# Decode attention: the first weight load is one of 16 rows on partitions 0 to 15

## The chip, the cores and the metric

The kernel runs on one core of one Trainium2 chip. The metric is the time of one execution in microseconds of device time. The median of three runs before the change was 1265.98 us (1265.68 to 1267.26).

## The reference

One token is decoded. Its row x of 448 numbers is used in two branches, which a gate mixes. Branch a is attention with a long cache: 16 query heads of 256 over 8 key/value heads with 65536 positions each. Branch b is a small MLP over a layer-normed x. All tensors are bf16.

```
g = sigmoid(sum(x * gate_w))
q = x @ wq                                  # 448 -> 16 heads of 256
p = softmax(q . k / 16)                     # two query heads share one key head, 65536 positions
a = (p @ v) @ wo                            # 4096 -> 448
u = gelu(layernorm(x)^T * w1 + b1)          # 448 x 1792
b = u @ w2 + b2
out = g * a + (1 - g) * b
```

The two caches are 268 MB each; everything else is under 8 MB. So nearly all traffic is keys and values, each of which is read once.

## The kernel before, in words

The work goes in 32 passes (`NP`), four for each key/value head. A pass covers 16384 positions: 8 MB of keys and 8 MB of values, laid out as 128 partitions of 64 KB. Keys go into `kring`, values into `vbuf`.

SyncE (`block.sync`) issues all large loads in one hand-written order, with waits on semaphores that say when a buffer is free. The DMA engines take its queue, q1, in that order. TensorE turns the keys of a pass around in 128x128 blocks (line 349, into the PSUM tile `kst`), ScalarE (line 797) and VectorE (line 657) copy the result to `ktT`, and TensorE multiplies it by the current query `qcur` (line 370). After the maxima and the exponentials, the values are summed up with the weights `pT` (line 401).

Ahead of the passes there is a short prologue. SyncE's first issues, in this order, are:

- line 256 (`load_wo(0)`): the output weights of the first key/value head, 128 rows of 3.5 KB, into `wo_sb`;
- line 259: `wq_a`, the first 384 rows of the query weights. Partition p gets rows 3p to 3p+2, one run of 24 KB;
- line 261: `wq_b`, the remaining 64 rows, as 128 runs of 4 KB;
- line 264, twice: the second and then the first half of the first keys, 128 runs of 32 KB each.

ScalarE issues six small loads on its own queue, q10: x, the gate weights, three parameter vectors of the MLP, and one bias. TensorE waits for both loads of query weights (`sem_wq`, line 490) and computes all queries (lines 497 and 499). `wq_a` and `wq_b` lie in the space of `vbuf`, so SyncE holds the first values back (lines 272 and 273) until the query projection and the broadcast of the layer-normed row are through. The output weights are first read after the fourth pass (line 462).

Of the kernel before, what the change touches and what calls it, by code (L numbers as in the profile page):

```python
# [12 lines left out]
def bass_gated_mix__gqa_block_cached__mixer_token_mlp__decode_kernel(  # L13
# [25 lines left out]
    P = 128  # L39
# [17 lines left out]
    WF = 3  # L57
# [38 lines left out]
    with ctx:  # L96
# [6 lines left out]
        def new_sem(name):  # L103
            return ctx.enter_context(nc.semaphore(name))
# [22 lines left out]
        wq_a = early[:, 0:WF * NQ].rearrange("p (j n) -> p j n", j=WF)  # L127
# [75 lines left out]
        sem_wq = new_sem("sem_wq")  # L203
# [43 lines left out]
        def src(cache, j, n0=0, n1=NV):  # L247
            g, m = divmod(j, PPH)
            s = cache[0, g, m * BODY * CH:(m + 1) * BODY * CH, :].rearrange("(p n) d -> p n d", p=P)
            return s[:, n0:n1, :].rearrange("p n d -> p (n d)")  # L250

        @block.sync
        def _(eng):
            def load_wo(g):
                w = A_wo[g * REP * DH:(g + 1) * REP * DH, :]
                eng.dma_start(wo_rows, w.rearrange("(p i) n -> p (i n)", i=2 * REP)).then_inc(sem_wo, 16)

            load_wo(0)
            eng.dma_start(wq_a.rearrange("p j n -> p (j n)"),
                          A_wq[0:WF * P, :].rearrange("(p j) n -> p (j n)", p=P)).then_inc(sem_wq, 16)  # L260
            eng.dma_start(wq_b, A_wq[WF * P:DM, :].rearrange("r (a n) -> (r a) n", a=2)
                          ).then_inc(sem_wq, 16)
            def load(dst, cache, j, n0, n1, at, sem):
                eng.dma_start(dst[:, at + n0:at + n1, :].rearrange("p n d -> p (n d)"), src(cache, j, n0, n1)  # L264
                              ).then_inc(sem, 16)

            load(kring, A_k_cache, 0, HV, NV, 0, sem_k)
            load(kring, A_k_cache, 0, 0, HV, 0, sem_kb)

            def load_v(j):  # L270
                if j == 0:
                    eng.wait_ge(s_q, 1)
                    eng.wait_ge(s_hb, 1)
                else:
                    eng.wait_ge(sem_pv, j)
                load(vbuf, A_v_cache, j, 0, NV, 0, sem_v)
                g, m = divmod(j, PPH)
                if m == 0 and 1 <= g < H - 1:
                    eng.wait_ge(s_proj, g)
                    load_wo(g)  # L280

            for j in range(NP):
                if j == LEAD + 1:
                    eng.wait_ge(sem_tr[NB - 1], BODY * LEAD)
                    load(kring, A_k_cache, j, HV, NV, HV, sem_kc[1])
                if j >= 1:
                    eng.wait_ge(sem_tr[NB - 1], BODY * (j - 1) + DC)
                if j == LEAD:
                    load(kring, A_k_cache, j, HV, NV, 0, sem_k)
                    load(kring, A_k_cache, j, 0, HV, 0, sem_kc[0])  # L290
                elif j == LEAD + 1:
                    load(kring, A_k_cache, j, 0, HV, HV, sem_k)
                elif j == NP - 1:
                    load(kring, A_k_cache, j, 0, HV, HV, sem_k)
                    load(kring, A_k_cache, j, HV, NV, HV, sem_kc[2])
                elif j >= 1:
                    load(kring, A_k_cache, j, 0, NV, HV * (j % 2), sem_k)
                if j < LEAD:
                    load_v(j)
                elif j > LEAD:  # L300
                    load_v(j - 1)


            for (n0, n1), sem in zip(pieces, sem_vp):
                if n0 == 0:
                    eng.wait_ge(sem_tr[NB - 1], BODY * (NP - 1))
                elif n0 == NRING:
                    eng.wait_ge(sem_pv, NP - 1)
                load(kring if n1 <= NRING else vbuf, A_v_cache, NP - 1, n0, n1, 0, sem)
            eng.wait_ge(s_proj, H - 1)  # L310
            for h in range(REP):
                w = A_wo[(HQ - REP + h) * DH:(HQ - REP + h + 1) * DH, :]
                eng.dma_start(wo_sb[:, h, :], w.rearrange("(p j) n -> p (j n)", j=2)).then_inc(sem_wl[h], 16)
            eng.wait_ge(s_fin, NCG)
            eng.dma_start(out_ap, out_row[:, :]).then_inc(sem_out, 16)
            eng.wait_ge(sem_out, 16)
# [13 lines left out]
        def _(pe):  # L330
# [95 lines left out]
            def piece_wait(n):  # L426
                for (n0, _), sem in zip(pieces, sem_vp):
                    if n == n0:
                        pe.wait_ge(sem, 16)
# [57 lines left out]
            pe.matmul(acc[:, WF + 2:WF + 2 + 3 * FT], wrows_b, identb, start=True, stop=True).then_inc(s_col, 1)  # L487

            pe.wait_ge(s_xcol, 1)
            pe.wait_ge(sem_wq, 32)  # L490
            for dj in range(2):
                for h in range(HQ):
                    j = dj * HQ + h
# [28 lines left out]
            with nc.Fori(0, NP + 1, 1, engines=on, head_slot={pe.engine: 0}) as jj:  # L522
                j = pe.snap(jj, min_val=0, max_val=NP)
# [312 lines left out]
```

## Time and profile before

| | |
|---|---|
| median of 3 runs | 1265.98 us |
| profiled execution: time / span | 1266.13 us / 1264.3 us |
| moved by DMA | 544.39 MB, mean 431 GB/s over the span |
| TensorE busy | 956.9 us (76%), mean granted clock 0.856 |
| ScalarE / VectorE busy | 544.5 us (43%) / 497.4 us (39%) |
| first query projection matmul | 12.97 us |
| first transposes of keys (line 349) | 24.04 us |
| first values issued by SyncE | 17.9 us |
| first output projection (line 462) | 202 us |

The time of an execution includes what lies outside of the span of instructions (1.8 us here). "Issue to landing" of a load runs from the moment that SyncE issues it to the moment that its semaphore is complete, so it includes the time that it stands behind earlier loads.

### The profile page before, as it was taken

The page shows a single profiled execution, that of the slowest core. Times are in us where ns is not written, and L with a number is a line of the kernel's source. Part 1 is how long each engine was busy: PE and PEld are TensorE (multiplying, and loading weights), DVE is VectorE, ACT ScalarE, POOL GpSimd, SP SyncE. Part 2 cuts the span into 40 slices and gives each one's busy share as a digit, 9 for nine tenths or more (in the row PEclk, how much of TensorE's full clock was granted, in tenths as well). Part 3 has the DMA queues.
Part 4 walks back from the last instruction along what each step waited for, and adds up shares of the span by engine and source line. Part 5 has one row for each costly group of instructions (what it writes and reads, how often), then busy time and mean ns, then how long its engine had stood idle before and what let it go on. Part 6 is the DMA issues. An engine that isn't in the chain of part 4 may idle for free.

```text
span 1264.3 us, 39978 instructions
## 1 busy us (share of the span) xinstructions
PE 956.9 (76%) x17201; PEld 881.7 (70%) x17201; DVE 497.4 (39%) x1125; ACT 544.5 (43%) x692; POOL 0.9 (0%) x7
## 2 busy tenths in 40 slices
PE   4778887678776787767877768886769867697786
PEld 3677876668766687666877667775668756687674
DVE  3333434444544444444344423342333423344342
ACT  2444543345533455334554334443344533345451
POOL 0000000000000000000000000000000000000000
PEclk9878887898888897788988889887888878898898
DMA  9999999999999999999999999999999999999998
GB/s 421 427 421 422 438 435 433 438 431 431 431 433 440 433 433 431 431 440 431 433 433 424 438 440 433 431 427 433 433 435 440 423 435 431 435 433 435 427 446 353
DMA packets 12055, 544.39 MB, mean 431 GB/s; under 512 B 1417, under 2 KB 1676, under 8 KB 2956
## 3 DMA queue, kind: packets, MB, share of 16 engines
q1 hardware_dynamic: 11954, 544.22, 99.7%
q8 instruction: 8, 0.13, 0.0%
q10 hardware_dynamic: 90, 0.01, 0.0%
q14 instruction: 3, 0.02, 0.0%
HBM read 544.22 MB, written 0.00 MB: 430 GB/s over the span
## 4 chain that ended last, share of the span: by engine, by line
DMA 63%; PE 34%; issue 1%; DVE 1%; DVEq 0%; SPq 0%; ACT 0%
DMA kring<-in_A_k_cache_dram 59%; PE kst L349 25%; PE sps L370 6%; DMA vbuf<-in_A_v_cache_dram 2%; PE acc L401 2%; DMA wo_sb<-in_A_wo_dram 1%; PE acc L451 0%; PE sps L389 0%; SPq L264 0%; PE acc L394 0%; DVE ktT L657 0%; PE sps L387 0%; ACT z_b L802 0%; DVE mrow L668 0%; DVE accs L691 0%
## 5 line engine op out<-in xcount | busy, mean ns | idle before, releaser
L349 PE MATMUL kst<-ident,kring 128*128 128x128 f32 x4096 | 557.2, 297 | 196.9 <-DMA kring<-in_A_k_cache_dram 173.1
L349 PEld LDWEIGHTS kst<-ident,kring 128*128 128x128 f32 x4096 | 505.5, 154 | 205.4 <-issue 199.9
L797 ACT ACTIVATE ktT<-kst 128x1024 bf16<-128x1024 bf16 x512 | 499.0, 1021 | 345.2 <-PE kst L349 344.5
L657 DVE COPY ktT<-kst 128x1024 bf16<-128x1024 bf16 x512 | 353.8, 692 | 440.3 <-PE kst L349 414.4
L370 PEld LDWEIGHTS sps<-qcur,ktT 128*128 128x128 bf16 x8192 | 237.8, 96 | 2.6
L370 PE MATMUL sps<-qcur,ktT 128*128 128x2 bf16 x8192 | 236.6, 163 | 0.0
L401 PE MATMUL acc<-vbuf,pT 128*2 128x256 bf16 x4024 | 158.3, 332 | 6.1 <-DMA vbuf<-in_A_v_cache_dram 3.4
L401 PEld LDWEIGHTS acc<-vbuf,pT 128*2 128x2 bf16 x4024 | 110.7, 101 | 45.8 <-issue 5.7
L780 ACT ACTIVATE fade<-mdif 128x2 f32<-128x2 f32 x32 | 6.5, 204 | 301.1 <-DVE mdif L674 301.1
L668 DVE TENSOR_REDUCE mrow<-sps 2x1 f32<-2x128 f32 x32 | 8.9, 279 | 158.9 <-PE sps L387 158.9
L387 PE MATMUL sps<-ident,mcol 128*2 128x128 f32 x32 | 8.9, 279 | 29.9 <-issue 23.4
L389 PEld LDWEIGHTS sps<-mdiag,mones 2*128 2x128 f32 x64 | 11.4, 221 | 27.9 <-DVE mdiag L670 27.9
L784 ACT ACTIVATE pT<-sps,mneg 128x64 f32 x128 | 30.4, 335 | 0.0
L389 PE MATMUL sps<-mdiag,mones 2*128 2x2 f32 x64 | 14.1, 288 | 21.3 <-DVE mdiag L670 21.3
L394 PE MATMUL acc<-pT,ones_sq 128*128 128x32 bf16 x256 | 11.9, 182 | 22.8 <-issue 19.3
L387 PEld LDWEIGHTS sps<-ident,mcol 128*2 128x2 f32 x32 | 2.6, 80 | 37.8 <-issue 28.1
L802 ACT ACTIVATE z_b<-z_b 128x448 bf16<-128x448 bf16 x14 | 8.1, 578 | 48.1 <-DVE z_b L644 48.1
L691 DVE COPY accs<-acc 128x288 f32<-128x288 f32 x8 | 3.7, 458 | 62.3 <-PE acc L401 62.3
L663 DVE TENSOR_REDUCE mcol<-sps 128x2 f32<-128x256 f32 x32 | 13.5, 423 | 35.4 <-PE sps L370 35.4
L394 PEld LDWEIGHTS acc<-pT,ones_sq 128*128 128x128 bf16 x256 | 8.8, 99 | 26.1 <-issue 22.5
L686 DVE TENSOR_SCALAR acc<-acc,fader 128x256 f32<-128x256 f32 x32 | 15.8, 493 | 2.5
L673 DVE TENSOR_SCALAR mneg<-sps 128x2 f32<-128x2 f32 x32 | 5.1, 160 | 17.1 <-PE sps L389 17.1
(108 smaller groups left out, 171.1 us busy)
## 6 DMA issues: line engine op xcount, KB each, us to landing
kring<-in_A_k_cache_dram SPq DMA_DIRECT2D x8, 4096.0 KB, 23.7
kring<-in_A_v_cache_dram SPq DMA_DIRECT2D x1, 3584.0 KB, 35.9
wo_sb<-in_A_wo_dram SPq DMA_DIRECT2D x7, 448.0 KB, 25.7
vbuf<-in_A_wq_dram SPq DMA_DIRECT2D x1, 3072.0 KB, 10.3
vbuf<-in_A_v_cache_dram SPq DMA_DIRECT2D x1, 2560.0 KB, 9.2
vbuf<-in_A_v_cache_dram SPq DMA_DIRECT2D x1, 1024.0 KB, 11.3
vbuf<-in_A_v_cache_dram SPq DMA_DIRECT2D x1, 768.0 KB, 12.8
vbuf<-in_A_wq_dram SPq DMA_DIRECT2D x1, 512.0 KB, 11.1
```

The lines of the kernel that those rows point to most:

```text
L349: ins = pe.transpose(kst[:, b, i * P:(i + 1) * P], kring_f[:, at + NT * (k % DC) + 4 * b + i, :], ident[:, :])
L370: ins = pe.matmul(sps[:, 0, 2 * (NT * k + nt):2 * (NT * k + nt) + 2], ktT[:, par, b, ntl * DH + dj:(ntl + 1) * DH:2], qcur[:, dj, :], star ...
L387: pe.transpose(mxT, mcol[:, :], ident[:, :]).then_inc(s_mT, 1)
L389: pe.matmul(mxB, mones[:, :], mdiag[:, :], start=True, stop=True).then_inc(s_mB, 1)
L394: pe.matmul(acc[:, DENC:SELC], ones_sq[:, :], pT[:, r, :], start=False, stop=(r == BODY - 1), skip_group_check=True)
L401: ins = pe.matmul(acc[o:o + REP, 0:DH], pT[:, r, 2 * nt:2 * nt + 2], buf[:, n, :], start=False, stop=False, skip_group_check=True)
L657: vec.tensor_copy(ktT[:, k % KTB, b, :], kst_b[:, b, :]).then_inc(sem_ev[b], 1)
L663: vec.tensor_reduce(out=mcol[:, :], in_=scores_all.rearrange("p (n hh) -> p hh n", hh=REP), axis=AX.X, op=ALU.max)
L668: vec.tensor_reduce(out=mrow[:, :], in_=mxT, axis=AX.X, op=ALU.max)
L686: vec.tensor_scalar(acc[:, 0:DENC], acc[:, 0:DENC], fader[:, :], None, op0=ALU.mult).then_inc(s_acc, 1)
L784: ins = act.activation(pT[:, bass.ds(p0, DC), hh:2 * NT:REP], scores_all.rearrange("p (a r n hh) -> p a hh r n", a=2, r=DC, hh=REP)[:, hal ...
L797: act.activation(ktT[:, k % KTB, b, :], kst_b[:, b, :], AF.Copy).then_inc(sem_ev[b], 1)
```

## The change

The load of `wq_a` is divided by partitions. The rows of partitions 0 to 15 (16 runs of 24 KB) are issued first of all. Then come the output weights, unchanged, and then the rows of partitions 16 to 127 (112 runs of 24 KB). All that follows keeps its order. `sem_wq` counts one load more, so TensorE waits for 48 instead of 32. Bytes, destinations and all other engines' programs stay as they are.

```
-            load_wo(0)
-            eng.dma_start(wq_a.rearrange("p j n -> p (j n)"),
-                          A_wq[0:WF * P, :].rearrange("(p j) n -> p (j n)", p=P)).then_inc(sem_wq, 16)
+            for p0, p1 in ((0, 16), (16, P)):
+                eng.dma_start(wq_a[p0:p1].rearrange("p j n -> p (j n)"),
+                              A_wq[WF * p0:WF * p1, :].rearrange("(p j) n -> p (j n)", j=WF)).then_inc(sem_wq, 16)
+                if p0 == 0:
+                    load_wo(0)
             eng.dma_start(wq_b, A_wq[WF * P:DM, :].rearrange("r (a n) -> (r a) n", a=2)
                           ).then_inc(sem_wq, 16)
...
-            pe.wait_ge(sem_wq, 32)
+            pe.wait_ge(sem_wq, 48)
```

## Prediction, made before the changed kernel had run

> **What bounds the kernel now.** I read the page's slices and DMA queues first, to see which resource is never idle. The columns of a queue line are packets, MB, and share of 16 engines.
>
> ```profile
> DMA  9999999999999999999999999999999999999998
> GB/s 421 427 421 422 438 435 433 438 431 431 431 433 440 433 433 431 431 440 431 433 433 424 438 440 433 431 427 433 433 435 440 423 435 431 435 433 435 427 446 353
> ...
> q1 hardware_dynamic: 11954, 544.22, 99.7%
> ```
>
> The 16 DMA engines are busy in every slice, and nearly all that they move is SP's queue, q1. Then I read stretches of the span (length, busy time and instructions of each engine, granted clock, DMA share, GB/s).
>
> ```profile
> 24.00:118.00 94.00, 72.02 (x1206) 65.44 (x1206) 32.43 (x62) 41.08 (x50) 0.00 (x0) 0.84 1.01 433
> 118.00:121.00 3.00, 2.64 (x49) 2.63 (x49) 1.38 (x2) 1.61 (x3) 0.00 (x0) 1.00 0.87 328
> 121.00:1240.00 1119.00, 863.40 (x15507) 800.22 (x15503) 452.03 (x1008) 497.27 (x630) 0.00 (x0) 0.86 1.00 433
> ```
>
> From 121 to 1240 us the share is 1.00 at 433 GB/s: 27.06 GB/s for each engine. TensorE is busy for 863.4 of those 1119 us, so it is not the bound. Only at 118 to 121 us do the queues run short (0.87, or 0.13 x 3 = 0.4 us of stream). The waits between 30 and 1260 us say the same from the other side: TensorE waits for keys, 28 times.
>
> ```profile
> ...
> PE kst L349 <- DMA kring<-in_A_k_cache_dram: 167.3, 28, 9.7
> ...
> ```
>
> So the end is: when the stream starts, plus bytes over 433 GB/s, plus a tail of 2.5 us (the chain of waits has the last landing at 1261.8 us, the span ends at 1264.3). The tail is not touched, nor is a byte added. What the change can do is shift the stream as a whole, and the place to read is its first few microseconds. Here are SP's issues, then the DMA of the first 4 us in slices of 0.1 us.
>
> ```profile
> 0.74 0.41 SPq L256 DMA_DIRECT2D wo_sb<-in_A_wo_dram  x1
> 1.20 0.41 SPq L259 DMA_DIRECT2D vbuf<-in_A_wq_dram  x1
> 1.67 0.42 SPq L261 DMA_DIRECT2D vbuf<-in_A_wq_dram  x1
> 2.13 0.97 SPq L264 DMA_DIRECT2D kring<-in_A_k_cache_dram  x2
> ```
>
> ```profile
> DMA  0000000000000000097924598899889999950000
> GB/s 0 0 0 0 0 0 0 0 0 0 0 0 0 0 0 0 9 179 143 251 72 143 215 358 323 287 394 394 287 358 430 466 1162 1837 983 246 0 0 0 0
> ```
>
> The first packets move in slice 17 (1.7 us), 1.0 us after the issue. Slices 17 to 30 are the output weights (128 rows of 3.5 KB, 459 KB): their figures add up to 3834, times 0.1 us is 383 KB in 1.4 us, where 433 GB/s would have moved 606 KB. This stuttering start costs 223 KB / 433 GB/s = 0.5 us. (A packet's bytes are counted where it starts, hence the peaks behind it.)
>
> **The change part by part.** *One more issue on SP.* An issue takes 0.41 us and the next follows 0.46 us later, so the remaining query weights, the remainder load and both key loads are issued 0.46 us later than now. Cover: key bytes cannot move before some 4.1 MB ahead of them (9.5 us at 433 GB/s) have gone, and they are issued at 2.13 us. Cost 0; without that cover, 0.46 us. The 16 rows go where the output weights stood at 0.74 us, so the stream's first packet stays at about 1.7 us.
>
> *Output weights moved behind the 16 rows.* Their first reader is the projection at 202 us. Cost 0.
>
> *What the stuttering start gives back.* Sixteen rows of 24 KB give each engine one packet of 24,576 B / 27.06 GB/s = 0.91 us, under which the small rows can be prepared. The gain lies between 0 (any first packet is as slow) and 0.5 us (all of it). I take half: -0.25 us.
>
> *The 16 rows as a load on partitions 0 to 15.* All loads of q1 in the trace write 128 partitions, so they can't say whose limit 27.06 GB/s is: the engine's, or that of the eighth of a 128-row load (8 partitions) that each engine fills. If it is the engine's, the 16 rows take 0.91 us and cost nothing. If it is the destination's, what counts is how many such groups of eight the partitions 0 to 15 reach: 16 groups if neighbours are spread as widely as possible (0.91 us, +0), 2 if neighbours lie together (8 rows in turn, 7.3 us, +6.4). Dealt evenly, which I assume, each engine has one of these rows first in its queue, so all 16 are held up, and what stands behind them waits. Neighbouring partitions are nearer to the dense end than to the spread one: I take 4 groups, 4 rows in turn, 3.64 us, +2.73 us.
>
> [...]
>
> *The other 112 rows.* [...] With the destination as the limit, two engines that meet in a group take 1.82 us for a row each instead of 0.91. Ends: they never meet (+0), or each of the seven rows meets another (+6.4 us). Four groups have lost 4 of their 8 rows to the first load, so the other twelve still hold 8 where the even share is 7: one row, 0.91 us, is lost at the least. [...] I take three meetings for the later engines, since a load lands with its slowest engine: +2.73 us.
>
> [...]
>
> *Who waits for this.* The semaphore threshold of 48 is the same wait for one load more. TensorE starts the query projection at 12.97 us; 5 us later it would end at 21.6 instead of 16.6, and SP would issue the first values at about 23 instead of 17.9 us. The keys ahead of them keep the engines busy until about 11 + 19.4 = 30.4 us (8.39 MB at 433 GB/s), later still when shifted. Cover 12 us; if it were gone, each us late would cost one. ScalarE's small loads take turns with these packets and may land some us later than 11.4; their chain ends in the same projection. TensorE's first transposes, at 24.04 us, wait for the first half of the keys and move with the stream.
>
> *Sum.* -0.25 + 2.73 + 2.73 = +5.2 us. The stream is full from there to the end, so nothing gives it back, except up to the 0.4 us of 118 to 121 us, which itself hangs on transposes that start with a key landing and so moves too. The profiled execution took 1266.13 us (span 1264.3), which becomes 1271.3; it lies 0.15 us above the median of 1265.98, so I forecast 1271.2 us. A measurement of this kernel can tell about 0.2%, 2.5 us, from no change.
>
> **Rivals.**
>
> *The limit is the engine's own (chance 0.19).* Then both loads go at 433 GB/s wherever they land, and what is left is the start: 0 to -0.5 us, 1265.7 us, not slower. For it: the rate is the same for every load in the trace. Against it: nothing in this trace, since no large load there writes fewer than 128 partitions. It decides if the 16 rows are through by about 2.9 us.
>
> *Only the 16 rows suffer (0.16).* If the 112 rows are dealt so that engines hardly meet, -0.25 + 2.73 = +2.5 us, 1268.5 us, right at the 0.2%; half of this I count as slower. It includes the case that the loads are not dealt one row and seven rows to an engine: 16 rows on four engines, four each, would also hold those four up by 2.73 us.
>
> *Dense groups (0.06).* Two groups instead of four: +6.4 for the first load and 2 to 4 for the second, 1274 to 1276 us.
>
> *The change hides anyway.* A delay of the first loads would vanish if TensorE were the bound later. Its idle time before the transposes (167.3 us, ended by the keys) speaks against it: the only slack is 0.4 us. It is inside the first rival's range.
>
> *Faster by over 0.2% (0.03).* All that there is to gain is 0.5 us of the start and 0.4 us at 118 us, together 0.07%; only something that the trace doesn't show would give more.
>
> **How the numbers follow.** The forecast's own case (both loads slowed) has 0.56, with 1268.8 to 1273.5 us. Slower by over 0.2%: 0.56 + 0.08 + 0.06 = 0.70. Faster: 0.03. Same: 0.19 + 0.08 = 0.27. The range that holds the time 8 times in 10 has to take in the second rival and most of the first, and the forecast's case up to the replay's slowest engine and a little over: 1265.5 to 1273.5 us. It leaves out the dense groups and a part of each tail.
>
> **What would show each step right or wrong.** In the first 4 us in slices: 16 packets of 24 KB at about 1.7 us and then no start of output weights before about 5 us (the limit is the destination's) or at about 2.7 us (it is the engine's). The DMA issue list: the remaining query weights land 10.3 us after their issue now; right would be some 15 us, wrong about 10. TensorE's first transposes on keys: 24.04 us now, about 29 if right, 23.8 if the first rival holds, 26.5 if the second. From there on all landings are shifted by the same amount to the end; if the shift of the transposes is there and the end doesn't have it, the claim that the stream never gives time back is wrong. DMA share in the rest of the span stays at 1.00. What would make the forecast wrong altogether is a first transpose at or before 24.0 us.

## The result, and the profile after

The changed kernel takes 1272.61 us (median of 6 runs, 1272.19 to 1273.15); beside it the kernel before took 1265.88 (6 runs). The ratio is 1.0048, 95% interval 1.0037 to 1.0058: 6.7 us more. The profiled execution took 1272.79 us with a span of 1271.0.

Where the time went is read from the start of the stream. First SyncE's issues (start and duration in us; from line 261 on, the lines of the new kernel are two further down):

```profile
0.74 0.39 SPq L259 DMA_DIRECT2D vbuf<-in_A_wq_dram  x1
1.18 0.41 SPq L256 DMA_DIRECT2D wo_sb<-in_A_wo_dram  x1
1.64 0.43 SPq L259 DMA_DIRECT2D vbuf<-in_A_wq_dram  x1
2.12 0.43 SPq L263 DMA_DIRECT2D vbuf<-in_A_wq_dram  x1
2.59 0.45 SPq L266 DMA_DIRECT2D kring<-in_A_k_cache_dram  x1
```

The 16 rows take the first place, and each later issue moves back by some 0.46 us. Then the DMA of the first 8 us, in slices of 0.2 us:

```profile
DMA  0000000099700000000019799693889999000599
GB/s 0 0 0 0 0 0 0 0 496 1352 123 0 0 0 0 0 0 0 0 0 18 126 72 112 125 72 179 72 233 323 376 430 1402 744 0 0 0 123 1107 614
...
vbuf<-in_A_wq_dram SPq DMA_DIRECT2D x1, 2688.0 KB, 16.4
...
wo_sb<-in_A_wo_dram SPq DMA_DIRECT2D x1, 448.0 KB, 6.2
vbuf<-in_A_wq_dram SPq DMA_DIRECT2D x1, 384.0 KB, 5.4
```

These are the two loads in the kernel before (size, issue to landing):

```profile
vbuf<-in_A_wq_dram SPq DMA_DIRECT2D x1, 3072.0 KB, 10.3
...
wo_sb<-in_A_wo_dram SPq DMA_DIRECT2D x1, 448.0 KB, 3.2
```

Both rows of the slices count a packet, its time and its bytes, where it starts. The 16 packets of 24 KB start between 1.6 and 2.2 us, and then no packet of the queue starts for 2 us: each engine sits on its first row, which takes 2.3 to 3.0 us by the trace's packet records. At 433 GB/s the 393 KB are worth 0.91 us. The output weights start at 4.0 to 4.2 us. Their issue to landing was 3.2 us and is 6.2 us. The remaining query weights land 16.4 us after their issue, where the undivided load took 10.3.

Next, three stretches in which the 112 rows alone are in motion. The last two columns are DMA share and GB/s; the same stretch of the kernel before follows in a second fence.

```profile
7.00:10.00 3.00, 0.00 (x0) 0.00 (x0) 0.00 (x0) 0.00 (x0) 0.00 (x0) 1.00 1.02 263
10.00:13.00 3.00, 0.00 (x0) 0.00 (x0) 0.00 (x0) 0.00 (x0) 0.00 (x0) 1.00 0.88 263
13.00:16.00 3.00, 0.00 (x0) 0.00 (x0) 0.00 (x0) 0.00 (x0) 0.00 (x0) 1.00 1.04 262
```

```profile
7.00:16.00 9.00, 3.24 (x114) 3.12 (x115) 2.47 (x12) 1.69 (x3) 0.00 (x0) 1.00 1.06 449
```

The engines are busy all the time (0.88 to 1.04) but move 263 GB/s instead of 433 to 449. A busy DMA engine is not a fast one. 16 x 24,576 B / 263 GB/s = 1.50 us for a row; the trace's records of the single packets have 1.42 us on the average, and none of the 112 below 1.1.

Later on the stream is as it was:

```profile
118.00:121.00 3.00, 3.00 (x54) 2.99 (x53) 1.69 (x4) 2.35 (x3) 0.00 (x0) 1.00 0.94 404
121.00:1240.00 1119.00, 875.17 (x15461) 808.65 (x15460) 451.12 (x1006) 496.93 (x630) 0.00 (x0) 0.85 1.00 434
```

```profile
...
PE kst L351 <- DMA kring<-in_A_k_cache_dram: 164.7, 29, 10.7
...
```

433 to 434 GB/s again, and TensorE still waits for keys. The delay stays to the end. These are the first transposes of keys, before and after (start, length):

```profile
24.04 6.55 PE L349 MATMUL kst<-ident,kring 128*128 128x128 f32 x32 [5.78 <-DMA kring<-in_A_k_cache_dram]
```

```profile
29.95 5.53 PE L351 MATMUL kst<-ident,kring 128*128 128x128 f32 x32 [5.31 <-DMA kring<-in_A_k_cache_dram]
```

And this is the last landing in the chain of waits, before and after:

```profile
1248.72 13.11 DMA wo_sb<-in_A_wo_dram
```

```profile
1255.64 12.88 DMA wo_sb<-in_A_wo_dram
```

The transposes begin 5.9 us later than before, and the last landing is 6.7 us later (1261.82 before, 1268.52 now).

### The profile page after: what moved, and what is told of

Its sections match the earlier page's. It is cut to its first block, busy times and chain, and to the rows that moved or that the text cites. A ratio compares the mean times of both kernels' runs of the same rounds, so it can differ in the third digit from the quotient of the medians.

```text
span 1271.0 us, 39979 instructions
## 1 busy us (share of the span) xinstructions
PE 968.6 (76%) x17201; PEld 889.1 (70%) x17201; DVE 497.4 (39%) x1125; ACT 544.9 (43%) x692; POOL 0.9 (0%) x7
## 4 chain that ended last, share of the span: by engine, by line
DMA 58%; PE 37%; issue 2%; DVE 2%; DVEq 1%; SPq 0%; ACT 0%
DMA kring<-in_A_k_cache_dram 55%; PE kst L351 26%; PE sps L372 6%; PE acc L403 3%; DMA vbuf<-in_A_v_cache_dram 2%; DMA wo_sb<-in_A_wo_dram 1%; PE acc L453 0%; PE sps L391 0%; DVE ktT L659 0%; ACT z_b L804 0%; PE acc L396 0%; PE sps L389 0%; DVE accs L693 0%; SPq L266 0%; DVE mrow L670 0%
## 5 line engine op out<-in xcount | busy, mean ns | idle before, releaser
L351 PEld LDWEIGHTS kst<-ident,kring 128*128 128x128 f32 x4096 | 510.8, 155 | 196.0 <-issue 189.9
L403 PE MATMUL acc<-vbuf,pT 128*2 128x256 bf16 x4024 | 163.7, 339 | 5.0 <-DMA vbuf<-in_A_v_cache_dram 2.7
## 6 DMA issues: line engine op xcount, KB each, us to landing
vbuf<-in_A_wq_dram SPq DMA_DIRECT2D x1, 2688.0 KB, 16.4
```

The source lines that it names most:

```text
L351: ins = pe.transpose(kst[:, b, i * P:(i + 1) * P], kring_f[:, at + NT * (k % DC) + 4 * b + i, :], ident[:, :])
L403: ins = pe.matmul(acc[o:o + REP, 0:DH], pT[:, r, 2 * nt:2 * nt + 2], buf[:, n, :], start=False, stop=False, skip_group_check=True)
```

## The experiments

The theory behind the forecast is called D below: the limit of 27 GB/s is at the destination, where neighbouring partitions share a way in. Its rivals: S, the reads collide at their source in HBM, the chip's memory; C, whatever comes first is slow. D does not say which partitions share a way in; groups of eight neighbours are an assumption that is held against the runs below. All comparisons are with runs of the kernel before on the same chip, so the medians of before differ (1266.2 to 1266.6 us). Durations of rows are those of the trace's packet records.

**The 16 rows alone, and where they land.** Four kernels load 16 rows first into a spare part of `vbuf`, then the output weights, then all 128 rows of query weights in one load. They differ in destination and source. The count that TensorE waits for is raised for the added load, here and wherever loads are added; the code shown leaves that out.

```
+            eng.dma_start(spare[DST, :], A_wq[0:WF * P, :].rearrange("(p j) n -> p (j n)", p=P)[SRC, :]
+                          ).then_inc(sem_wq, 16)
             load_wo(0)
             eng.dma_start(wq_a ..., all 128 rows)
# e1_dense: DST 0:16, SRC 0:16      e2_dst_step8: DST 0:P:8, SRC 0:16
# e3_src_step8: DST 0:16, SRC 0:P:8 e4_dst_step7: DST 0:106:7, SRC 0:16
```

> The 16 rows of 24 KB go first, to a spare part of vbuf on partitions 0 to 15, which nobody reads; then come the output weights and all 128 rows of query weights in one load. So the 112-row load is gone, and 393 KB are moved twice (0.9 us at 433 GB/s). Theory D (the limit is at the destination: neighbouring partitions share a way in): the 16 rows land 5.4 us after their issue as in the changed kernel, the rest goes at full rate, time 3.2 us above the kernel before, 1269.1 us. Theory S (the limit is at the source: 16 runs that lie side by side in HBM are read at once): the same here. Theory C (a first load of any kind is slow): the same here. If the 112 rows cost nothing, the time would be that of the changed kernel, 1272.6, plus 0.9.

> As e1_dense, but the 16 rows go to partitions 0, 8, 16 ... 120; the source is the same 16 neighbouring runs. D: the rows meet less, the load lands 3.3 to 4.2 us after its issue instead of 5.4, time 1267 to 1268 us. [...] S and C: no change, 5.4 us and 1269.1 us.

> As e1_dense, with the destination on partitions 0 to 15 again, but the 16 runs are taken from every eighth place of the query weights. D: no change, landing at 5.4 us, 1269.1 us. S: landing at about 3.3 us, 1267 us. C: 5.4 us, 1269.1 us.

> As e2_dst_step8, but to partitions 0, 7, 14 ... 105. [...] D with groups of eight neighbours (16 rows reach 14 groups, two of them twice): slightly more than in e2_dst_step8. S and C: as e1_dense, 1269.1 us.

Measured: the issue to landing of the 16 rows, in the order e1, e2, e3, e4:

```profile
vbuf<-in_A_wq_dram SPq DMA_DIRECT2D x1, 384.0 KB, 5.6
```

```profile
vbuf<-in_A_wq_dram SPq DMA_DIRECT2D x1, 384.0 KB, 4.1
```

```profile
vbuf<-in_A_wq_dram SPq DMA_DIRECT2D x1, 384.0 KB, 5.7
```

```profile
vbuf<-in_A_wq_dram SPq DMA_DIRECT2D x1, 384.0 KB, 3.8
```

The landing follows the destination (5.6 dense, 4.1 on every eighth, 3.8 on every seventh partition) and not the source (5.7 when the source is spread). A row took 2.32, 1.45, 2.44 and 1.12 us on the average. That rules out S and C as the main cause. Groups of eight neighbours would have made e2 the best of all, but its rows took 1.32 to 1.66 us, those of e4 0.91 to 1.37. This alone is thin, since e5 below shows a first round that is slow in a load of all 128 partitions too (1.64 us a row); e10 and e11 say more. Which partitions share a way in is not shown. The times are 1268.84, 1268.16, 1269.28 and 1268.10 us against 1266.61 (ratios 1.0016, 1.0010, 1.0019, 1.0010, each to within 0.0010). So the extra 16 rows cost 2.2 us when dense (3.2 were expected), 0.9 of which are bytes: the first load alone does not explain 6.7 us. In e1 the 128 rows behind it took 0.91 to 0.94 us each in the mean of a round, so nothing lingers. e4 came out level with e2: its 16 rows were shorter, but in its next rounds single rows took up to 2.07 us, and the last packet of query weights ends at 15.4 us in e4 and at 15.3 in e2.

**What does not matter.** The whole load first; the same 393 KB cut by columns; the 16 rows behind the output weights; the 112 rows from another source.

```
# e5_whole_first: wq_a (128 rows), load_wo(0), wq_b
# e8_columns: early[:, 0:WF*NQ//8] (128 rows of 3 KB), load_wo(0), early[:, WF*NQ//8:WF*NQ]
# e6_wo_first: load_wo(0), wq_a[0:16], wq_a[16:128]
# e9_src_keys: as the changed kernel, the second load from
+                    w = A_k_cache[0, 0].rearrange("(p n) d -> p (n d)", n=NV)[p0:p1, 0:WF * NQ]
```

> The query weights of all 128 partitions go first, in one load of 128 rows of 24 KB, then the output weights; nothing is divided. Theory D (neighbouring partitions share a way in): no row meets another, the first packets take 0.9 us plus a start of up to 0.4 us, and the stuttering start of the output weights is covered: 0 to 0.5 us below the kernel before. Theory C (what comes first is slow): the first 16 packets take 2.3 us or more again, 1 us or more above the kernel before.

> The same 393 KB ahead of the output weights, but taken as 3 KB from each of the 128 partitions instead of 24 KB from each of 16; the other 21 KB of each follow as the second load. Every partition is reached by both loads. D: within 0.5 us of the kernel before. If a divided load or one more issue cost the time, the 6.7 us would stay.

> The division into 16 and 112 partitions stays, but the output weights are first again. D: nothing depends on being first; the 16 rows hold the engines up for some 1.7 to 2.7 us wherever they stand, the 112 rows as before; 6.2 to 7.2 us above the kernel before. If the place at the head were the cause: less than 4 us above.

> As the changed kernel, but the 112 rows of the second load are read from the keys at a pitch of 64 KB instead of from the query weights at 24 KB (so most of the queries are made of the wrong weights). In the changed kernel each of those rows took 1.42 us on the average instead of 0.91, and all engines alike. D (seven neighbouring rows to an engine, which meet others' at the destination): 1.3 to 1.5 us again, 6.2 to 7.2 us above the kernel before. S (the reads collide at the source's pitch): 0.9 to 1.0 us a row, about 3.5 us less than the changed kernel.

Measured, before at 1266.23 us: e5 1266.84 (ratio 1.0006, 0.9997 to 1.0015), e8 1266.14 (1.0001, 0.9991 to 1.0010), e6 1273.13 (1.0055, 1.0040 to 1.0071), e9 1272.17 (1.0046, 1.0031 to 1.0061). A divided load with one more issue was free where both parts reach all 128 partitions (e8). Being first is not the cause (e6: 6.9 us). And the 112 rows are as slow from another place and pitch in HBM (e9: 5.9 us, a little under the 6.2 to 7.2 expected):

```profile
7.00:10.00 3.00, 0.00 (x0) 0.00 (x0) 0.00 (x0) 0.00 (x0) 0.00 (x0) 1.00 1.01 263
10.00:13.00 3.00, 0.00 (x0) 0.00 (x0) 0.00 (x0) 0.00 (x0) 0.00 (x0) 1.00 0.89 263
```

e5 is a partial miss of D. It has no row meet another there, yet nothing is gained. The first 8 us in slices of 0.2 us:

```profile
DMA  0000000099543500499852959299582999229552
GB/s 0 0 0 0 0 0 0 0 250 1106 123 123 123 246 0 0 123 492 737 369 246 123 983 246 492 123 493 867 246 369 124 620 617 494 124 124 1233 246 246 123
```

Eleven packets start by 2.0 us, the other five of the first round (123 GB/s in a slice is one packet) trickle in up to 2.8 us, and the second round begins at 3.2 us. The first 16 rows took 1.64 us on the average instead of 0.91, the following 112 rows 0.92. So this start is slow where D has no rows meet, and C holds for up to 0.7 us, but not for the rest.

**Why all 112 rows are slow.** All engines were slow alike: none of the 112 rows took less than 1.1 us. The expectations call it theory N that any load whose rows are not dealt as in a 128-row load is slow; by D it matters which partitions are written at the same time. Two kernels move the same bytes, four loads of 16 rows, onto every fourth partition (from 32 on) or every seventh (from 0 on). Two more divide the 128 rows by halves and by parity.

```
             load_wo(0)
+            for o in OFFSETS:
+                eng.dma_start(spare[o:o + 15 * ST + 1:ST, :], rows[o:o + 15 * ST + 1:ST, :]).then_inc(sem_wq, 16)
             eng.dma_start(wq_a ..., all 128 rows)
# e10_four_step4: ST 4, OFFSETS 32, 33, 34, 35     e11_four_step7: ST 7, OFFSETS 0, 1, 2, 3
# e7_half:   load_wo(0), partitions 0:64, then 64:128
# e12_parity: load_wo(0), partitions 0:127:2, then 1:128:2
```

> The output weights first, then four loads of 16 rows of 24 KB to a spare part of vbuf, each on every fourth partition from 32 (33, 34, 35) on, then all query weights in one load. 1.57 MB are moved in addition, 3.6 us at 433 GB/s. [...] Theory N (any load whose rows are not dealt as in a 128-row load is slow, met or not): 1.2 us a row or more, 5 us above or more.

> [...] N: the same as e10_four_step4.

> The output weights first, then the query weights as two loads of 64 partitions, 0 to 63 and 64 to 127. [...] N: the same as for the 112 rows, 1.42 us a row, 4.1 us above.

> As e7_half, but the two loads take the even and the odd partitions. [...]

Measured, before at 1266.50 us: e10 1272.34 (ratio 1.0045, 1.0029 to 1.0062), e11 1274.02 (1.0057, 1.0040 to 1.0074), e7 1275.65 (1.0072, 1.0056 to 1.0089), e12 1268.19 (1.0015, 1.0005 to 1.0024). The stretch from 6 to 8 us of each, in the order e10, e11, e7, e12 (last columns DMA share, GB/s):

```profile
6.00:8.00 2.00, 0.00 (x0) 0.00 (x0) 0.00 (x0) 0.00 (x0) 0.00 (x0) 1.00 0.93 371
```

```profile
6.00:8.00 2.00, 0.00 (x0) 0.00 (x0) 0.00 (x0) 0.00 (x0) 0.00 (x0) 1.00 1.05 261
```

```profile
6.00:8.00 2.00, 0.00 (x0) 0.00 (x0) 0.00 (x0) 0.00 (x0) 0.00 (x0) 1.00 1.04 210
```

```profile
6.00:8.00 2.00, 0.00 (x0) 0.00 (x0) 0.00 (x0) 0.00 (x0) 0.00 (x0) 1.00 0.97 409
```

The engines are as busy in all four, at 371, 261, 210 and 409 GB/s. Halves run at half of 433 GB/s: rows of 1.78 to 1.95 us in all but the first of eight (two rows of 0.91 in turn would be 1.82). In e10 the rows come down from 1.48 through 1.18 and 1.09 to 0.96 us, the slow start again, and stay at 0.91 to 0.92. That is against N. In e11, with the same bytes in four loads again, they go from 1.36 and 1.18 up to 1.58, 1.47 and 1.34 us, and only then to 1.00 and 0.92. (The 1.34 is the first round of the undivided load behind the four. A slow row seems to hold up the next: in e6 the 16 rows took 2.2 to 3.3 us and the first round of the 112 behind them still 2.44 on the average, the later ones 1.37 to 1.65.)

None of the 32 rows of e11's third and fourth load is below 1.3 us, and the engines were busy throughout (share 1.05 at 6 to 8 us): every row of these loads was held up, not a few. That does not show from the first packet: in e4 7 of the 16 rows took 0.91 to 1.05 us, and 4 rows of e11's first two loads 0.91 to 0.92. What holds the rows up, and when, these runs don't show. That the 112 rows are slow for the same reason is inferred, from the same rate (261 and 263 GB/s) and the same evenness; how their rows are dealt was not seen.

Three results stand apart. e12 was not slow like e7: its rows run at full rate (0.92 us in most rounds after the first two), save that one engine seems to fall behind: a row takes 2.41 us, and the last eight 4 KB packets of the query weights follow one another up to 14.5 us, when the rest are through by 13.0. Groups of eight neighbours would fit e12 if an engine takes four neighbours of the list, which was not seen; but they fail on the pair before: by them all rows of e10 meet and only 4 of 16 in each load of e11, and e10 is the faster one (371 against 261 GB/s). So why halves are slow and the even and the odd partitions are not is not shown; that was not tested further. e7 cost 9.2 us where N has 4.1: its eight rows cost an engine 7.2 us more than before, and the 4 KB rows behind them took 0.31 instead of 0.16 us each, 1.2 us more. e11 cost 7.5 where N has it level with e10 (5.8): its rows account for 6.0, and not all of the rest is placed.

A total is read from the slowest engine and from its own execution. The last packet of query weights ends at 12.4 us before; it ends later by 6.2 us in the changed kernel, and by 3.1, 5.0, 7.3, 10.2 and 2.1 in e1, e10, e11, e7 and e12. The spans of the same executions are longer by 6.7, 3.3, 4.4, 7.9, 9.5 and 1.9 us: within 0.8 us in each. The mean of the first 16 packets of keys would say 0.2 for e12, since it leaves out what is late. e10's profiled execution was the fastest of its four (1270.55 us; the median is 5.8 us above before), so by its total alone e10 would speak for N (5 us above or more); its rows decide.

## Why the prediction was right, point by point

- *What bounds the kernel.* Right. The stream carries the shift to the end, 6.2 us at the last packet of query weights and 6.7 at the last landing. The half microsecond between is not placed; it is of the size of what the totals above leave open (0.8).
- *The 16 rows with the start given back, -0.25 + 2.73 = +2.48 us.* Right in sum, in part by luck. No run shows the four groups, four rows in turn, behind the 2.73 us; what was measured is 2.3 to 3.0 us for a row, 2.6 in the mean, instead of 3.64. The last packet of the output weights ends at 3.5 us before and at 6.7 now; of these 3.2 us 0.9 are the bytes moved ahead: +2.3 us. The part of -0.25 us has no support: e5 covers the small rows with large ones and gains nothing (1.0006). Without it the 2.73 is 0.4 us too dear, and the two errors offset each other in part. (The prediction calls the 8 partitions of an engine the eighth of a 128-row load; they are a sixteenth, and its sums use 8.)
- *The 112 rows, +2.73 us.* Right that the destination slows these rows (263 GB/s here and, read from the keys, in e9, where e8 onto all 128 partitions costs nothing), at too low a price. The first packets of the keys start at 12.1 us before and at 18.2 now (mean of the first 16), +6.1, which leaves 3.8 us for this part. The step that failed is the count of three meetings for the later engines, a term that no run shows: the rows of all engines took 1.42 us on the average and none below 1.1, and 7 x (1.42 - 0.91) = 3.6 us.
- *Who waits for this.* Right. SyncE issued the first values at 24.3 us (17.9 before), a little later than the 23 forecast, and the cover was still there.
- *The rivals.* The engine's own limit is refuted by e1 to e4 (1.12 to 2.44 us a row, by destination) and e7 (210 GB/s). "Only the 16 rows suffer" is refuted by the 263 GB/s. Dense groups: two groups were to cost +6.4 us for the 16 rows, four +2.73; they cost 2.3.
- *What would show it.* The output weights were to start at about 5 us and started at 4.1; a row's 2.6 us (1.68 above 0.91) is less than four full turns of 0.91, and the remainder shows in the output weights' own packets, which took 0.27 us on the average instead of 0.19. The remaining query weights landed at 16.4 us for "some 15", the transposes began at 29.95 for "about 29".
- Sum: 1271.2 us forecast, 1272.61 measured; +5.2 against +6.7 us, within the forecast case's own 1268.8 to 1273.5. No run shows the replay that its upper end was taken from; the last packet of query weights ended 6.2 us later.

## What to carry to other kernels

Divide a load along the columns, not along the partitions: in this stream, which is bound by DMA, 16 + 112 partitions cost 6.7 us, 64 + 64 cost 9.2 us, and the even and the odd ones 1.7 us, where 128 partitions twice cost nothing (e8, ratio 1.0001). A DMA share near 1.00 does not say that the engines run at their rate; read the GB/s beside it (1.04 at 210 GB/s in e7). And in this saturated stream what was lost in the prologue (5.9 us at the first transposes) was paid at the end (6.7 us at the last landing), so the first loads are worth the same care as the loop.

## What the runs showed of the hardware

- 16 rows of 24 KB onto partitions 0 to 15 take 2.3 to 2.6 us each in the mean (e1, e3, the changed kernel); onto every eighth partition 1.45 (e2), onto every seventh 1.12 (e4), and in steady loads of 128 partitions 0.91.
- Rows onto 16 partitions that lie seven apart, loaded four times in turn, moved at 261 GB/s with all engines busy (share 1.05 in e11), and the 112 neighbouring rows at 263, where partitions four apart came to 0.91 to 0.92 us a row (e10) and undivided loads run at 433. The reason is not shown.
- The first packets of the queue are slow in a load of all 128 partitions too: 24 KB rows took 1.64 us on the average in e5. No order that was tried gained anything: ratio 1.0006 in e5, 1.0001 in e8.
